# Token transform in 64-row array tiles, one gate product, grouped small VectorE operations and a second recurrence PSUM buffer in a gated spectral/state-space kernel

## The chip, the cores and the metric

The kernel runs on one core of a Trainium2 chip. The core has a matrix engine (TensorE, PE in the profile; its weight loads are PEld), VectorE (DVE), ScalarE (ACT), GpSimd (POOL) and SyncE (SP, which here only issues DMAs). Compute engines read and write SBUF, 128 partitions wide; TensorE writes PSUM, which has 8 banks of 2 KB per partition. The metric is device time in microseconds (us).

## The reference, cut to what matters

```python
S, D = 2048, 1024                      # tokens, channels (batch 1, bf16)
g = sigmoid((x * gate_w).sum(-1))      # one gate per token
a = irfft2(rfft2(x) * (w_r + 1j*w_i))  # 2-D transform over tokens and channels
Lb = exp(exp(log_dt) * (Lambda_re + 1j*Lambda_im))         # 1024 states
Bu = x @ (((Lb - 1)/Lam)[:, None] * (B_re + 1j*B_im)).T
h[t] = Lb * h[t-1] + Bu[t]                                 # 2048 steps
b = 2*real(h @ (C_re + 1j*C_im).T) + x * Dskip
out = g*a + (1 - g)*b
```

The weights `w` have 513 columns, and the transform's column 0 carries the real sums of the two ends of the spectrum packed together, so it takes a small path of its own.

## The kernel before

**Two branches on one instruction stream.** The source is an order written out by hand: the instructions of TensorE, VectorE and ScalarE run in the order in which the Python code issues them, and a generator for each branch is stepped so that the two interleave.

**Front (iterations j = 0 to 15, function `front`).** The token rows are dealt to 128 partitions as token = 16·p + j, so tile j holds the tokens with residue j modulo 16. For each j, `turn_x` transposes the tile by eight matmuls into a one-bank PSUM tile `pt` (L647), and ScalarE copies it into `xQ` (L648). `fold` adds and subtracts its halves on VectorE (L652, L653), `fd` does the channel transform by eight 512-column matmuls (L335), ScalarE copies that out as `X1` (L338), and `s1` does the token transform over the 128 partitions by four matmuls of 512 columns (L344 to L347). VectorE (j below 10) or ScalarE (later) copies the result out as `A1`, one of four buffers (L349), a DMA writes it to DRAM scratch, and VectorE keeps its column 0 in `Acol` (`keep_A1`, L356). The transposes run ahead and end with j = 6. Meanwhile `make_tab` builds the rotation tables on VectorE, ScalarE and GpSimd, and the loads of B and C are issued on SyncE.

**Recurrence (`unit(c, q)`).** Time is cut in 8 chunks c of 256 tokens, the states in halves q. A unit is two steps ("halves", real and imaginary part) of 32 matmuls of 256 columns each (L300, stationary operand B, moving operand columns of `xQ`), each evacuated by ScalarE into `h` (L302). Then VectorE works on the unit: rotate back (L261, L262), join (L267, L268, carry at L270), two scans (L274), carry on (L280 to L282), rotate on (L286, L287, L292, L293). These pieces go into a list, and `vector(us)` issues as many of them as a budget written in the code allows. `early(tb)` multiplies finished states with C for a tile of 128 tokens (L561, with the skip product at L565), ScalarE scales by 1 - g (L579), and the result goes to DRAM. The units and early tiles follow the list `ssm`; from j = 8 on, each front iteration takes one half.

**PSUM.** `psA` (two buffers of two banks) serves the transform. In the front, `psF` (one buffer of two banks) holds the recurrence product and `psX` (two buffers of one bank) the transposes and the gate. After j = 15 both are closed and `psU` (two buffers of two banks) takes the place of both.

**Gate.** At j = 9, 11, 13 and 15, `gate` forms four token tiles' gate sums, 32 matmuls of one column each (L689, stationary operand `xQ`), ScalarE copies four columns (L691), and at the end two GpSimd DMAs bring them to the token order (L693, L695). `gate_end` applies the sigmoid (L699) and makes g and 1 - g (L700 to L705).

**Behind the front.** `Acol` goes to DRAM and back as `Bcol` by two GpSimd DMAs (L362, L365); four 16-column matmuls (L410 to L413) do the rest of column 0's transform. Then 16 steps of the second token stage (L453), the product with w (L461, L462 on VectorE), and the way back (L477, L478), each with one half of the recurrence; then 16 steps of L502, and at last the channel transform back (L592) with the remaining units and the output tiles (`own`, `late_tile`).

Of the kernel before, what the change touches and what calls it, by code (L numbers as in the profile page):

```python
# [13 lines left out]
FP32 = mybir.dt.float32  # L14
# [5 lines left out]
S = 2048  # L20
# [16 lines left out]
def _host_consts():  # L37
# [21 lines left out]
    s1 = np.arange(P)[:, None, None]  # L59
    s2 = np.arange(16)[None, :, None]  # L60
    m1 = np.arange(P)[None, None, :]
    angT = 2 * np.pi * (((16 * s1 + s2) * m1) % S) / S
    Tc, Ts = np.cos(angT), np.sin(angT)
    p = np.arange(P)
    q = p // 8
    a = p % 8
    angK = 2 * np.pi * ((q[:, None] * q[None, :]) % 16) / 16
    delta = (a[:, None] == a[None, :]).astype(np.float64)
    Kc, Ks = delta * np.cos(angK), delta * np.sin(angK)
    f = np.arange(P)  # L70
    fs, fr, fa = f[:, None] // 8, (f[:, None] // 4) % 2, f[:, None] % 4
    hr, hm, ha = f[None, :] // 64, (f[None, :] // 4) % 16, f[None, :] % 4
    angF = 2 * np.pi * ((fs * hm) % 16) / 16
# [14 lines left out]
    for h in range(2):  # L88
# [10 lines left out]
        T3=b16(np.stack([Tc, Ts, -Ts], axis=2)),  # L99
        K3=b16(np.stack([Kc, Ks, -Ks], axis=1)),  # L100
# [7 lines left out]
def kernel(  # L108
# [24 lines left out]
    cT3 = nc.inline_tensor(hc["T3"], name="c_T3").ap()  # L133
# [7 lines left out]
    turn1_dram = dram.tile([16, 2, P, K], BF16, name="turn1_scratch")  # L141
    turn2_dram = dram.tile([32, P, K], BF16, name="turn2_scratch")
    col0_dram = dram.tile([P, 16, 2], BF16, name="col0_scratch")
    z_dram = dram.tile([P, 16], FP32, name="z_scratch")
# [47 lines left out]
    fft["T3"] = raw.rearrange("p (j t m) -> p j t m", t=3, m=P)  # L192
# [4 lines left out]
    def load_T3(a, b):  # L197
        nc.sync.dma_start(out=fft["T3"][:, a:b], in_=cT3[:, a:b])

# [50 lines left out]
    work = []  # L250

    def unit(c, q):
# [24 lines left out]
        def carry_on():  # L277
            if c + 1 < NCH:
                gl = u[:, :, :, TC - 1]
                nc.vector.tensor_mul(out=ck[:, 0, :, js], in0=gl, in1=cTC[:, js].unsqueeze(1).to_broadcast([P, 2, 4]))  # L280
                nc.vector.tensor_mul(out=ck[:, 1, :, js], in0=gl[:, ::-1], in1=sTC2[:, :, js])
                nc.vector.tensor_add(out=carry[:, :, js], in0=ck[:, 0, :, js], in1=ck[:, 1, :, js])  # L282
# [13 lines left out]
        for ri in range(2):  # L296
            psu = pools["u"].tile([P, 4, TC], FP32, name="psu", tag="psu")
            for j in range(4):
                for d8 in range(8):
                    nc.tensor.matmul(psu[:, j, :], lhsT=BT[4 * q + j][:, ri, d8, :],  # L300
                                     rhs=xQ[:, d8, :, 16 * c:16 * (c + 1)], start=(d8 == 0), stop=(d8 == 7))
            nc.scalar.copy(out=u[:, ri].rearrange("p b (q j) -> p b q j", j=16),  # L302
                           in_=psu.rearrange("p b (j q) -> p b q j", j=16))
            if ri == 1:
                work.extend([(2.4, turn_back), (1.5, join), (2.3, lambda: scan(0)), (2.3, lambda: scan(1)),
                             (0.5, carry_on), (2.4, turn), (1.4, join_on)])
            yield 3.5
# [19 lines left out]
    def gfnet():  # L327
        T3_sb, G_sb = fft["T3"], fft["G"]
        Acol = fx.tile([P, 16, 2], BF16, name="Acol")
# [11 lines left out]
        def s1(j):  # L341
            X1 = X1s.pop(j)
            psa = psA.tile([P, 2, K], FP32, name="ps_s1", tag="ps")
            nc.tensor.matmul(psa[:, 0, :], lhsT=T3_sb[:, j, 0, :], rhs=X1[:, 0, :], start=True, stop=False)  # L344
            nc.tensor.matmul(psa[:, 0, :], lhsT=T3_sb[:, j, 1, :], rhs=X1[:, 1, :], start=False, stop=True)
            nc.tensor.matmul(psa[:, 1, :], lhsT=T3_sb[:, j, 0, :], rhs=X1[:, 1, :], start=True, stop=False)
            nc.tensor.matmul(psa[:, 1, :], lhsT=T3_sb[:, j, 2, :], rhs=X1[:, 0, :], start=False, stop=True)  # L347
            A1 = gta.tile([P, 2, K], BF16, name="A1", bufs=4)
            (nc.vector.tensor_copy if j < 10 else nc.scalar.copy)(out=A1, in_=psa)  # L349
            A1s[j] = A1  # L350
            nc.sync.dma_start(out=turn1_dram[j].rearrange("r m k -> m r k"), in_=A1)
            if j:
                keep_A1(j - 1)

        def keep_A1(j):
            nc.vector.tensor_copy(out=Acol[:, j, :], in_=A1s[j][:, :, 0])  # L356
# [4 lines left out]
        keep_A1(15)  # L361
        nc.gpsimd.dma_start(out=col0_dram, in_=Acol)  # L362
        Bcol = fx.tile([P, 16, 2], BF16, name="Bcol")
        with nc.allow_non_contiguous_dma(reason="tiny corner turn"):
            nc.gpsimd.dma_start(out=Bcol, in_=col0_dram.rearrange("(a b) j c -> j a b c", a=8))  # L365
# [4 lines left out]
        Kc_sb, Ks_sb, Kns_sb = fft["K3"][:, 0], fft["K3"][:, 1], fft["K3"][:, 2]  # L370
        Wc = fft["Wc"]
        KRS_sb = fft["KRS"]
        t1_v = turn1_dram.rearrange("j r (a b) k -> (j r a) b k", a=4)
# [34 lines left out]
        yield "w"  # L408
        zps = psA.tile([P, 2, 16], FP32, name="zps", tag="ps")
        nc.tensor.matmul(zps[:, 0, :], lhsT=Kc_sb, rhs=Bcol[:, :, 0], start=True, stop=False)  # L410
        nc.tensor.matmul(zps[:, 0, :], lhsT=Ks_sb, rhs=Bcol[:, :, 1], start=False, stop=True)
        nc.tensor.matmul(zps[:, 1, :], lhsT=Kc_sb, rhs=Bcol[:, :, 1], start=True, stop=False)
        nc.tensor.matmul(zps[:, 1, :], lhsT=Kns_sb, rhs=Bcol[:, :, 0], start=False, stop=True)  # L413
# [94 lines left out]
    def after_ia():  # L508
# [7 lines left out]
        fft["wp"] = bctx.enter_context(tc.tile_pool(name="wp", bufs=1, side="right", reuse_waits="tile"))  # L516
        fft["Sel"] = fft["gt"].tile([P, 4, P], BF16, name="Sel_sb", tag="gc1", bufs=2)
# [126 lines left out]
    def turn_x(j):  # L644
# [3 lines left out]
        nc.scalar.copy(out=xQ[:, :, j, :], in_=pt)  # L648
# [6 lines left out]
    idle = gta.tile([P, K], BF16, name="idle", tag="A1", bufs=4)  # L655
# [11 lines left out]
    load_T3(0, 2)  # L667
    load_x(1)
    load_x(2)
    load_T3(2, 8)  # L670
    for i in range(3, 8):
        load_x(i)
    load_T3(8, 16)
# [8 lines left out]
    zsb = cpool.tile([P, 16], FP32, name="zsb")  # L682
    zt = cpool.tile([P, 16], FP32, name="zt")

    def gate(r0, n):
        zps = psX.tile([P, n], FP32, name="zps_g", tag="pt")
        for r in range(r0, r0 + n):
            for d8 in range(8):
                nc.tensor.matmul(zps[:, r - r0:r - r0 + 1], lhsT=xQ[:, d8, r, :], rhs=gwT[:, d8:d8 + 1],  # L689
                                 start=(d8 == 0), stop=(d8 == 7))  # L690
        nc.scalar.copy(out=zsb[:, r0:r0 + n], in_=zps)  # L691
        if r0 + n == 16:
            nc.gpsimd.dma_start(out=z_dram, in_=zsb)  # L693
            with nc.allow_non_contiguous_dma(reason="gate by token tiles"):
                nc.gpsimd.dma_start(out=zt, in_=z_dram.rearrange("(t a) j -> (a j) t", a=8))  # L695
# [14 lines left out]
    fft["K3"] = fx.tile([P, 3, P], BF16, name="K3_sb")  # L710
# [3 lines left out]
    def load_small():  # L714
        nc.sync.dma_start(out=fft["K3"], in_=cK3)
# [28 lines left out]
    def halves(gen, n):  # L744
        for _ in range(n):
            next(gen, None)

    ssm = chain(unit(0, 0), unit(0, 1), unit(1, 0), unit(1, 1),
                unit(2, 0), early(0), unit(2, 1), early(1), unit(3, 0), early(2), unit(3, 1), early(3),
                unit(4, 0), early(4), unit(4, 1), early(5), unit(5, 0), early(6), early(7), unit(5, 1),  # L750
                early(8), unit(6, 0), early(9))

# [208 lines left out]
```

## Time and profile before

Four runs took 347.52 to 353.04 us, median 350.13. The profiled execution took 344.79 us, its span is 343.0 us; the remaining 1.79 us lie around the span.

| what | value |
|---|---|
| profiled execution, its span | 344.79 us, 343.0 us |
| TensorE busy | 330.8 us (96%), granted clock 1.00 |
| VectorE busy | 292.4 us (85%) |
| ScalarE busy | 167.6 us (49%) |
| token transform, L344 to L347 | 64 matmuls of 512 columns |
| gate, L689 | 128 matmuls of 1 column |
| recurrence product, L300 | 1024 matmuls of 256 columns, 116.1 us busy |
| column copies L356 | 16, mean 159 ns |
| carry L280, L281, L282 | 14 each, means 165, 159 and 167 ns |
| diagonal L878 | 8, mean 245 ns |

A matmul's listed duration (379 ns at 512 columns, 273 at 256) is longer than its share of the engine, since matmuls overlap; the distance from one start to the next is what a matmul costs in a stream. A wait named in the profile belongs to the engine that waited, and idle time of an engine that is not the bound costs nothing.

### The profile page before, as it was taken

The page shows a single profiled execution, that of the slowest core. Times are in us where ns is not written, and L with a number is a line of the kernel's source. Part 1 is how long each engine was busy: PE and PEld are TensorE (multiplying, and loading weights), DVE is VectorE, ACT ScalarE, POOL GpSimd, SP SyncE. Part 2 cuts the span into 40 slices and gives each one's busy share as a digit, 9 for nine tenths or more (in the row PEclk, how much of TensorE's full clock was granted, in tenths as well). Part 3 has the DMA queues.
Part 4 walks back from the last instruction along what each step waited for, and adds up shares of the span by engine and source line. Part 5 has one row for each costly group of instructions (what it writes and reads, how often), then busy time and mean ns, then how long its engine had stood idle before and what let it go on. Part 6 is the DMA issues. An engine that isn't in the chain of part 4 may idle for free.

```text
span 343.0 us, 6408 instructions
## 1 busy us (share of the span) xinstructions
PE 330.8 (96%) x2496; PEld 218.6 (64%) x2529; DVE 292.4 (85%) x477; ACT 167.6 (49%) x215; POOL 35.2 (10%) x66
## 2 busy tenths in 40 slices
PE   8989899989999999999999999999999999999995
PEld 3555377667877684756657474595958885665552
DVE  2659777999997999999999999999546999999951
ACT  3698777663332126655656452365633343434410
POOL 1372111100021000000000000000000002112220
PEclk9999999999999999999999999999999999999999
DMA  7999999998874045889999953995501009845694
GB/s 261 414 260 188 219 208 213 189 259 195 265 175 87 8 94 139 235 217 249 268 254 278 233 155 105 240 227 130 160 0 63 1 11 177 153 109 87 113 159 149
DMA packets 83742, 59.55 MB, mean 174 GB/s; under 512 B 54368, under 2 KB 74496, under 8 KB 83584
## 3 DMA queue, kind: packets, MB, share of 16 engines
q1 hardware_dynamic: 80400, 56.46, 63.8%
q0 software_dynamic: 3232, 2.67, 8.0%
q8 instruction: 20, 0.33, 0.4%
q14 instruction: 10, 0.08, 0.1%
q10 hardware_dynamic: 80, 0.01, 0.0%
HBM read 31.32 MB, written 17.84 MB: 143 GB/s over the span
## 4 chain that ended last, share of the span: by engine, by line
PE 82%; ACT 6%; DVE 6%; issue 3%; DMA 2%; SPq 0%; ACTq 0%; DVEq 0%
PE psu L300 30%; PE ps_y L561 26%; PE ps_fd L335 4%; PE ps_h L561 4%; PE ps_id L592 4%; PE ps_is L477 2%; PE ps_is L502 2%; PE ps_is L478 2%; DMA G_sb<-c_G 2%; PE ps_y L565 2%; PE ps_s L453 2%; ACT xQ L648 1%; ACT X L338 1%; ACT h L302 1%; PE pt L647 1%
## 5 line engine op out<-in xcount | busy, mean ns | idle before, releaser
L300 PE MATMUL psu<-xQ,BT 128*128 128x256 bf16 x1024 | 116.1, 273 | 2.0 <-ACT zsb L691 1.0
L300 PEld LDWEIGHTS <-BT 128*128 128x128 bf16 x1024 | 99.5, 98 | 17.7 <-issue 2.9
L561 PE MATMUL ps_y<-CT,h 128*128 128x512 bf16 x436 | 99.5, 379 | 0.6
L561 PEld LDWEIGHTS <-h 128*128 128x128 bf16 x512 | 49.5, 98 | 55.3
L274 DVE TENSOR_TENSOR_SCAN h<-rz,h 128x1024 bf16<-128x1024 f32 x32 | 72.4, 2282 | 0.3
L302 ACT CAST h<-psu 128x1024 bf16<-128x1024 f32 x32 | 32.3, 1010 | 58.5 <-PE psu L300 58.5
L607 POOL DMA_DIRECT2D BT<-y_scratch x10 | 12.1, 1206 | 212.6 <-ACT BT L595 178.7
L335 PE MATMUL ps_fd<-G_sb,preT 128*128 128x512 bf16 x119 | 29.6, 379 | 2.4 <-ACT X L338 1.6
L579 ACT ACTIVATE ye<-ps_y,omg 128x512 f32<-128x512 f32 x20 | 12.6, 683 | 33.1 <-PE ps_y L565 22.7
L261 DVE TENSOR_TENSOR su<-h,tab 128x2048 bf16<-128x2048 bf16 x16 | 19.6, 1223 | 8.0 <-ACT h L302 5.4
L335 PEld LDWEIGHTS <-preT 128*128 128x128 bf16 x128 | 11.9, 97 | 15.3 <-issue 2.7
L455 ACT CAST X<-ps_s 128x1024 bf16<-128x1024 f32 x16 | 16.2, 1014 | 8.7 <-PE ps_s L453 8.7
L262 DVE TENSOR_TENSOR h<-h,tab 128x2048 bf16<-128x2048 bf16 x16 | 19.6, 1225 | 0.8
L338 ACT CAST X<-ps_fd 128x1024 bf16<-128x1024 f32 x16 | 16.2, 1012 | 8.2 <-PE ps_fd L335 6.7
L287 DVE TENSOR_TENSOR h<-h,tab 128x2048 bf16<-128x2048 bf16 x16 | 19.6, 1225 | 0.5
L286 DVE TENSOR_TENSOR sg<-h,tab 128x2048 bf16<-128x2048 bf16 x16 | 19.5, 1218 | 0.0
L504 ACT CAST ZT<-ps_is 128x1024 bf16<-128x1024 f32 x16 | 15.4, 1022 | 5.2 <-issue 3.0
L648 ACT COPY xQ<-pt 128x1024 bf16<-128x1024 bf16 x16 | 15.9, 1019 | 1.7 <-PE pt L647 1.7
L349 DVE CAST A<-ps_s 128x1024 bf16<-128x1024 f32 x10 | 12.2, 1220 | 5.2 <-PE ps_s L347 5.2
L480 ACT CAST C<-ps_is 128x1024 bf16<-128x1024 f32 x16 | 16.1, 1007 | 0.0
L592 PE MATMUL ps_id<-raw,ZT 128*128 128x256 bf16 x128 | 15.9, 273 | 0.0
L561 PE MATMUL ps_h<-CT,h 128*128 128x512 bf16 x62 | 14.4, 379 | 0.1
(192 smaller groups left out, 388.6 us busy)
## 6 DMA issues: line engine op xcount, KB each, us to landing
y_scratch<-ye SPq DMA_DIRECT2D x20, 256.0 KB, 2.7
CT<-in_A_x_dram SPq DMA_DIRECT2D x8, 512.0 KB, 6.1
turn_scratch<-A SPq DMA_DIRECT2D x16, 256.0 KB, 3.2
Bb<-turn_scratch SPq DMA_DIRECT2D x16, 256.0 KB, 4.0
turn_scratch<-C SPq DMA_DIRECT2D x16, 256.0 KB, 2.9
raw<-turn_scratch SPq DMA_DIRECT2D x16, 256.0 KB, 3.9
Wb<-in_A_w_r_dram SPq DMA_DIRECT2D x32, 127.8 KB, 4.0
Wb<-in_A_w_i_dram SPq DMA_DIRECT2D x32, 127.8 KB, 3.7
```

What stands on the lines that cost most here:

```text
L261: nc.vector.tensor_mul(out=su, in0=u[:, ::-1], in1=bc(1))
L262: nc.vector.tensor_mul(out=u, in0=u, in1=bc(0))
L274: nc.vector.tensor_tensor_scan(out=seg, data0=rz[:, js].rearrange("p j t -> p (j t)"), data1=seg, initial=0.0, op0=ALU.mult, op1=ALU.add)
L286: nc.vector.tensor_mul(out=sg, in0=u[:, ::-1], in1=bc(3))
L287: nc.vector.tensor_mul(out=u, in0=u, in1=bc(2))
L300: nc.tensor.matmul(psu[:, j, :], lhsT=BT[4 * q + j][:, ri, d8, :], rhs=xQ[:, d8, :, 16 * c:16 * (c + 1)], start=(d8 == 0), stop=(d8 == 7))
L302: nc.scalar.copy(out=u[:, ri].rearrange("p b (q j) -> p b q j", j=16), in_=psu.rearrange("p b (j q) -> p b q j", j=16))
L335: nc.tensor.matmul(ps[:, cls, :], lhsT=preTs[j][:, 4 * cls + d4, :], rhs=G_sb[:, cls, d4, :], start=(d4 == 0), stop=(d4 == 3))
L338: nc.scalar.copy(out=X1.rearrange("p r (i c) -> p r i c", c=2), in_=ps.rearrange("p c (r i) -> p r i c", r=2))
L561: nc.tensor.matmul(psy, lhsT=hs[c, jb // 4][:, ri, jb % 4, P * tq:P * (tq + 1)], rhs=CT[ri][:, jb, 512 * dh:512 * (dh + 1)], start=(i == 0 ...
L592: nc.tensor.matmul(pse[:, slot, :], lhsT=ZT_t[:, i, tb, :], rhs=fft["Gi"][:, i, :], start=(kb == 0), stop=(kb == 1))
L648: nc.scalar.copy(out=xQ[:, :, j, :], in_=pt)
```

## The change

**Token transform.** The 2048-point transform over tokens is split 32 x 64 where it was 16 x 128. `turn_x` writes `xQ` with the partition order (p = 2·q + g) sorted as g·64 + q, so the two halves of the partitions hold two residue classes. `s1` still issues four 512-column matmuls for a j, but each contracts over 64 partitions, rows 0 to 63 for g = 0 and 64 to 127 for g = 1 (`tile_position` (0, 0) and (64, 0)), into two PSUM banks. The real and imaginary output share the 128 columns. The constants shrink from three to two 128-column blocks for each j. The recurrence reads `xQ` with runs of 8 elements (16 bytes) where it read runs of 16.

**A1.** The four buffers become one tile with four slots; ScalarE copies from j = 8 on. `keep_A1` copies column 0 of all four slots at once, at j = 4, 8, 12 and behind the front; it is issued behind the copy of the next j, so its first slot then holds the tile of the next group.

**Column 0.** The way of `Acol` over DRAM is replaced by a transpose on TensorE (32 output partitions), two VectorE operations and 16 matmuls of 16 columns over 32 partitions.

**Gate.** One product at j = 10: the gate weights are spread to 32 columns, and 32 matmuls of 512 columns write four 32-partition strips of one bank (`tile_position` (0, 32·i)). ScalarE copies 512 columns, and the two DMAs follow at once; the first reads 4 partitions in pieces of 16 bytes.

**VectorE.** The carry takes two operations where it took three, the diagonal one where it took eight.

**Order.** `psF` and `psX` are closed after j = 11 and `psU` opened there. In `ssm`, `unit(5, 1)` comes before `early(7)`, and `unit(6, 1)` is taken in behind `unit(6, 0)`, ahead of `early(8)` and `early(9)`.

```diff
 def s1(j):
-    nc.tensor.matmul(psa[:, 0, :], lhsT=T3_sb[:, j, 0, :], rhs=X1[:, 0, :], start=True, stop=False)
-    nc.tensor.matmul(psa[:, 0, :], lhsT=T3_sb[:, j, 1, :], rhs=X1[:, 1, :], start=False, stop=True)
-    nc.tensor.matmul(psa[:, 1, :], lhsT=T3_sb[:, j, 0, :], rhs=X1[:, 1, :], start=True, stop=False)
-    nc.tensor.matmul(psa[:, 1, :], lhsT=T3_sb[:, j, 2, :], rhs=X1[:, 0, :], start=False, stop=True)
-    A1 = gta.tile([P, 2, K], BF16, name="A1", bufs=4)
-    (nc.vector.tensor_copy if j < 10 else nc.scalar.copy)(out=A1, in_=psa)
+    for r in range(2):
+        for g in range(2):
+            half = slice(64 * g, 64 * (g + 1))
+            nc.tensor.matmul(psa[:, g, :], lhsT=T2_sb[half, j, r, :], rhs=X1[half, r, :],
+                             start=(r == 0), stop=(r == 1), tile_position=(64 * g, 0))
+    A1 = A1_4[:, j % 4]
+    (nc.vector.tensor_copy if j < 8 else nc.scalar.copy)(out=A1, in_=psa)
...
-    if j:
-        keep_A1(j - 1)
+    if j % 4 == 0 and j:
+        keep_A1(j - 4)
...
 def keep_A1(j):
-    nc.vector.tensor_copy(out=Acol[:, j, :], in_=A1s[j][:, :, 0])
+    nc.vector.tensor_copy(out=Acol[:, :, j:j + 4].rearrange("p g j -> p j g"), in_=A1_4[:, :, :, 0])
...
-keep_A1(15)
-nc.gpsimd.dma_start(out=col0_dram, in_=Acol)
...
-    nc.gpsimd.dma_start(out=Bcol, in_=col0_dram.rearrange("(a b) j c -> j a b c", a=8))
+keep_A1(12)
...
+aps = psA.tile([32, P], BF16, name="aps", tag="ps")
+nc.tensor.transpose(out=aps, in_=Acol.rearrange("p g j -> p (g j)"), identity=ident)
+nc.vector.tensor_copy(out=Bcol[:, 0:2].rearrange("j c a b -> j (c a b)"), in_=aps)
+nc.vector.tensor_scalar_mul(out=Bcol[:, 2], in0=Bcol[:, 0], scalar1=-1.0)
+yield "a"
...
+    for i in range(8):
+        lhs, r = parts[i // 4]
+        nc.tensor.matmul(zps[:, c, :], lhsT=lhs[:, i % 4, :], rhs=Bcol[:, r, i % 4, :], start=(i == 0), stop=(i == 7))
...
+x_t = xQ.rearrange("p d j (g q) -> p d g j q", g=2)
...
-    rhs=xQ[:, d8, :, 16 * c:16 * (c + 1)], start=(d8 == 0), stop=(d8 == 7))
+    rhs=x_t[:, d8, :, :, 8 * c:8 * (c + 1)], start=(d8 == 0), stop=(d8 == 7))
...
-nc.scalar.copy(out=xQ[:, :, j, :], in_=pt)
+nc.scalar.copy(out=xQ[:, :, j, :].rearrange("p d (g q) -> p d g q", g=2), in_=pt.rearrange("p d (q g) -> p d g q", g=2))
...
-def gate(r0, n):
-    zps = psX.tile([P, n], FP32, name="zps_g", tag="pt")
-    for r in range(r0, r0 + n):
-        for d8 in range(8):
-            nc.tensor.matmul(zps[:, r - r0:r - r0 + 1], lhsT=xQ[:, d8, r, :], rhs=gwT[:, d8:d8 + 1],
-                             start=(d8 == 0), stop=(d8 == 7))
+def gate():
+    zps = psX.tile([P, K], FP32, name="zps_g", tag="pt")
+    for d8 in range(8):
+        for i in range(4):
+            nc.tensor.matmul(zps[32 * i:32 * (i + 1), :], lhsT=gw32[:, d8, :], rhs=xQ[:, d8, 4 * i:4 * (i + 1), :],
+                             start=(d8 == 0), stop=(d8 == 7), tile_position=(0, 32 * i))
...
+        nc.gpsimd.dma_start(out=z_dram.rearrange("(n i j) -> i n j", i=4, j=4),
+                            in_=zsb[0:P:32, :].rearrange("i (n j) -> i n j", j=4))
+        nc.gpsimd.dma_start(out=zt, in_=z_dram.rearrange("(t p) -> p t", p=P))
...
-nc.vector.tensor_mul(out=ck[:, 0, :, js], in0=gl, in1=cTC[:, js].unsqueeze(1).to_broadcast([P, 2, 4]))
-nc.vector.tensor_mul(out=ck[:, 1, :, js], in0=gl[:, ::-1], in1=sTC2[:, :, js])
-nc.vector.tensor_add(out=carry[:, :, js], in0=ck[:, 0, :, js], in1=ck[:, 1, :, js])
+nc.vector.tensor_mul(out=ck[:, :, :, js], in0=gl.unsqueeze(1).to_broadcast([P, 2, 2, 4]), in1=rot[:, :, :, js])
+nc.vector.tensor_add(out=carry[:, :, js], in0=ck[:, :, 0, js], in1=ck[:, :, 1, js])
...
-for d8 in range(8):
-    nc.vector.tensor_scalar_mul(out=fft["dgD"][:, d8, :], in0=ident, scalar1=dskT[:, d8:d8 + 1])
+nc.vector.tensor_mul(out=fft["dgD"], in0=ident.unsqueeze(1).to_broadcast([P, 8, P]),
+                     in1=vecT[:, 3].unsqueeze(2).to_broadcast([P, 8, P]))
...
-            unit(4, 0), early(4), unit(4, 1), early(5), unit(5, 0), early(6), early(7), unit(5, 1),
-            early(8), unit(6, 0), early(9))
+            unit(4, 0), early(4), unit(4, 1), early(5), unit(5, 0), early(6), unit(5, 1), early(7),
+            unit(6, 0), unit(6, 1), early(8), early(9))
...
-    if j in (9, 11, 13, 15):
-        gate(2 * (j - 9), 4)
+    if j == 10:
+        gate()
...
+    if j == 11:
+        xctx.close()
+        pools["u"] = ctx.enter_context(tc.tile_pool(name="psU", bufs=2, space=PSUM, reuse_waits="tile"))
```

## The prediction

> **What bounds the kernel now.** The page first: busy shares, then the chain of work that ended last.
>
> ```profile
> PE 330.8 (96%) x2496; PEld 218.6 (64%) x2529; DVE 292.4 (85%) x477; ACT 167.6 (49%) x215; POOL 35.2 (10%) x66
> ...
> PE 82%; ACT 6%; DVE 6%; issue 3%; DMA 2%; SPq 0%; ACTq 0%; DVEq 0%
> ```
>
> TensorE is busy for 96% and carries 82% of the chain. But the share is a mean over stages, so the busy time of each engine by stretch comes next (after the stretch and its length: PE, PEld, DVE, ACT, POOL, each with its instruction count, then granted clock, DMA share, GB/s).
>
> ```profile
> 20.00:30.00 10.00, 8.66 (x69) 4.99 (x69) 7.50 (x29) 9.06 (x13) 6.90 (x11) 1.00 1.14 188
> 30.00:40.00 10.00, 8.91 (x58) 4.62 (x58) 7.80 (x19) 9.23 (x14) 2.20 (x4) 1.00 1.10 207
> ...
> 60.00:70.00 10.00, 8.95 (x85) 5.97 (x85) 9.93 (x18) 6.78 (x13) 2.19 (x4) 1.00 1.08 203
> ...
> 160.00:180.00 20.00, 19.89 (x133) 12.59 (x134) 19.54 (x26) 11.89 (x19) 0.00 (x0) 1.00 0.98 260
> ```
>
> From 20 to 40 us ScalarE is the fullest engine (9.06 and 9.23 of 10), ahead of TensorE. From 40 us on TensorE has no gaps worth naming, so there a microsecond of matmuls saved is a microsecond of span. VectorE is nearly as full (19.54 of 20), so it must keep pace. TensorE's own waits up to 130 us, and its order of time around the 12th front iteration, name the gaps (start, length, what, count, and in brackets the idle time before):
>
> ```profile
> PE ps_fd L335 <- ACT X L338: 1.6, 2, 1.3
> ...
> PE psu L300 <- ACT zsb L691: 1.0, 1, 1.0
> ```
>
> ```profile
> 65.50 0.94 PE L689 MATMUL zps_g<-vecT,xQ 128*128 128x1 bf16 x32
> 66.31 1.89 PE L335 MATMUL ps_fd<-G_sb,preT 128*128 128x512 bf16 x7
> 68.03 0.38 PE L344 MATMUL ps_s<-X,raw 128*128 128x512 bf16 x1
> 68.25 0.38 PE L345 MATMUL ps_s<-X,raw 128*128 128x512 bf16 x1
> 68.46 0.38 PE L346 MATMUL ps_s<-X,raw 128*128 128x512 bf16 x1
> 68.68 0.38 PE L347 MATMUL ps_s<-X,raw 128*128 128x512 bf16 x1
> 70.08 3.65 PE L300 MATMUL psu<-xQ,BT 128*128 128x256 bf16 x32 [1.02 <-ACT zsb L691]
> ```
>
> Starts 0.216 us apart are what a 512-column matmul costs in a stream (the listed 0.38 overlaps the next). The last line is a wait for the one recurrence buffer. Everything below is measured against the profiled execution, 344.79 us (343.0 of span and 1.79 around it).
>
> **Token transform (s1).** Before, four matmuls are 4 x 0.216 = 0.86 us for a j. After, four again, each on half of the rows; whether the two halves run at the same time no row here shows. If they do, a j takes 2 x 0.216 = 0.43 us, if not 0.86. Each j also enters and leaves another shape of the array. One row has such a change, the five 8-row transposes of the small vectors (L787), which the program places in a 32-row tile:
>
> ```profile
> 8.34 0.59 PE L335 MATMUL ps_fd<-G_sb,preT 128*128 128x512 bf16 x2
> 8.87 0.28 PE L787 MATMUL vps<-ident,vec 8*128 8x8 bf16 x5
> 9.07 0.39 PE L335 MATMUL ps_fd<-G_sb,preT 128*128 128x512 bf16 x1
> ```
>
> The last L335 before it starts at 8.34 + 0.59 - 0.38 = 8.55, so the next start was due at 8.77 and came at 8.87: 0.10 late. The fifth transpose starts near 8.99 and L335 follows at 9.07, about 0.06 more than their own spacing of 0.03. I take 0.16 us for a way in and out. Then s1 costs 0.43 + 0.16 = 0.59, saving 0.27 a j. Ends: 0.43 saved (free change, both halves at once), 0.16 lost (one after the other). I take 0.27, because the shape change is the measured row, and half of the array idle is the reason for such a tile.
>
> The Trainium skill speaks against the saving: the page "TensorEngine Tiling (Array Packing)", section "Tiling Modes", states that a change of tiling mode drains the engine. Taken as the overlap lost each way, 0.379 - 0.216 = 0.163 us, a j would pay 0.33 and save 0.10, and the forecast below would lose 16 x 0.17 = 2.7 us; L787 shows half of that, so I stay with the row.
>
> Eight of the sixteen lie in the front's ScalarE-bound part. There 8 x 0.27 = 2.2 us are offered; ScalarE idles 0.94 + 0.77 = 1.7 us from 20 to 40, and some of that is waiting for TensorE. I count 0.8 (ends 0 and 2.2). The other eight give 2.2.
>
> **Gate.** The four blocks take 0.80 us each (65.50 to 66.31): 3.2 us. The new product is 32 matmuls of 512 columns. Four strips at once make 8 x 0.216 + 0.16 = 1.9 us, a saving of 1.3; one after the other 32 x 0.216 + 0.16 = 7.1, a loss of 3.9. I take 1.3, by the same choice as for s1. The page "TensorE: Matmul & The Clock Gate", Part 3, reports 3.07 times for four row tiles of 512 columns; 32 x 0.216 / 3.07 would make 2.3 and the saving 0.8.
>
> **Column 0.** Four small matmuls (0.03 apart, 0.1 us) become 16 and a transpose (0.5 + 0.06) with two changes of shape (0.32): 0.8 us lost, ends 0.4 and 1.0. The two GpSimd DMAs that go were long done when needed.
>
> **Waits.** The 1.02 us at 70.08 and 0.24 at 87.80 are for the one recurrence buffer. The new pool's first buffer lies on the old one's banks, so the step at j = 12 waits for the same copy; but the gate's product now stands before it, and by my walk through the order the copy is done by then. In exchange A1 for j = 8 moves into ScalarE's queue ahead of the first h copy (0.9 us by L349's row), which ended at 48.7 while TensorE reached the next step at 49.04. That step would now be ready at 48.5 and wait until about 49.7, 1.2 us. Behind A1 stand the table operations and h in ScalarE's queue, and VectorE's first unit waits for h. Together: 0.1 us gained, ends -1 and +1.3.
>
> **VectorE** is off the end's path as long as it keeps pace, and the margin is thin:
>
> ```profile
> 131.99 0.69 DVE L462 TENSOR_TENSOR X<-X,Wb 128x1024 bf16<-128x1024 bf16 x1
> ```
>
> TensorE needs this product at 133.79 (first L477), 1.1 us after it ends. VectorE gains the 1.72 us that it waits for the sigmoid at 108 (the gate's DMAs now land 30 us earlier), about 0.75 at the first unit (it starts at 55.22 on an h copy that a late table operation holds up; A1 of j = 9 no longer stands in front of that), five carries of 0.09, five column copies of 0.07, 0.2 on the diagonal, and pays 0.25 for Bcol: 3.2, with the front's 0.8 about 4.0. TensorE comes 3.6 earlier, so the cover holds. If it didn't, TensorE would wait at L477. The two GpSimd gate DMAs now stand ahead of the last table copies (L220, L226), which turn_back of the second unit waits for. Issue 0.6 and 1.2, landing 4.0 by their rows, copies 1.4 and 0.8: done near 73, needed near 75.
>
> **Order at the end.** `unit(6, 1)` moves ahead of 14 us of early tiles. It fills VectorE's two idle spells of 5.2 and 5.4 us at 245 to 260, in which TensorE was busy anyway. Nothing waits on VectorE there, so I count 0. The DMA volume falls by 0.5 MB in the front; TensorE waited there only 0.7 us for a load of x; 0.
>
> **The sum.** 0.8 + 2.2 + 1.3 - 0.8 + 0.1 = 3.6 us: 341.2 of 344.79, ratio 0.990. The median of the runs before is 350.13, 1.5% above the profiled one; with the ratio it becomes **346.5 us**. Runs of this kernel lie up to 0.8% on either side of their median; 2% is about what a measurement can tell from no change.
>
> **Rivals.**
>
> *Slower: the tiles run one after the other.* Place: s1 and the gate. Price: 16 x 0.16 + 3.9 + 0.8 = 7.3 us, 352.1, by the ratio 357.5. It decides when a j of s1 takes over 0.90 us (0.86 plus a sixteenth of what the gate then leaves). For it: no row shows two tiles at once. Against: the matmuls alternate between the tiles and write different banks. 0.14.
>
> *Slower: the 16-byte runs.* The recurrence product reads runs of 8 elements. 32 matmuls take 3.49 us with runs of 16, 0.109 each, and the contiguous 256-column L592 takes the same (8 in 0.875), so halving the run from whole to 16 cost nothing, which speaks against. Each nanosecond would cost 1.02 us; at 0.120 the time is 344.79 - 3.6 + 11.3 = 352.5, by the ratio 357.9. "SBUF — State Buffer", section "Door 1: The DMA port swizzle", puts lines at 16 bytes and asks two hits in each, which a run of 8 bf16 meets; no run here shows it. 0.10.
>
> *Faster: shape changes are free.* 16 x 0.43 + 1.5 - 0.4 + 1.3 = 9.3 us, 335.5, by the ratio 340.7. Against: L787, ScalarE in the front, and VectorE, which by its own gain and margin lets only 4.0 + 1.1 = 5.1 us through (344.9). 0.28.
>
> *VectorE takes over.* GpSimd's table copies come 3 us late or the h copies slip, VectorE's gain falls to about 1, and TensorE waits at L477: 1.0 + 1.1 let through, 348.0. 0.10.
>
> **Chances.** Forecast 0.38. Within 2%: 0.38 + 0.10 = 0.48. Faster by over 2%: 0.28. Slower: 0.14 + 0.10 = 0.24. The range runs from the fast rival less some run spread, 339.5, to the slow ones' centre, 357.6, which leaves out about half of these and little below. The forecast's own range is 343 to 349.
>
> **What would show it.** L348's starts in pairs, then 0.59 us from one j's first to the next work; the gate near 1.9 us; L300 still 0.109; TensorE busy near 327; the sigmoid's wait gone; a wait of about 1 us at the second recurrence step; no wait at the first is1. It would be wrong if the tiles don't overlap, if L300 slows, or if VectorE's first unit starts later than now.

## The result

The changed kernel took 347.58 us (median of 44 runs, 345.42 to 349.81), the kernel before, over 71 runs, 346.18 us (344.68 to 353.04). The ratio is 1.0046, with a 95% interval of 1.0032 to 1.0060: half a per cent slower, where the forecast was 0.990. Ratios here and below leave out runs over 1.5% above the fastest of their kernel, most of which are of the kernel before, so they are not the quotients of the medians. That the forecast time, 346.5 us, lies near the measured one is luck: it was scaled from a median of four runs, 350.13, and from the 346.18 of the 71 runs the same ratio gives 342.6. The profiled execution has a span of 345.3 us, before 343.0.

**TensorE works less and waits more.** The busy shares and the chain of the changed kernel's page, the lines that answer to the first two of before:

```profile
PE 326.3 (94%) x2414; PEld 211.9 (61%) x2446; DVE 289.9 (84%) x447; ACT 169.9 (49%) x214; POOL 33.0 (10%) x64
...
PE 72%; DVE 17%; ACT 5%; SPq 2%; issue 2%; DMA 1%; DVEq 0%; ACTq 0%
```

TensorE's busy time fell from 330.8 to 326.3 us, by 4.5. Its idle time, span less busy, rose from 12.2 to 19.0, by 6.8. The difference is the 2.3 us of span. (Both profiles lack 32 or 33 matmul records; profiles with all of them, of experiments 4 and 1 below, show 332.9 and 328.5 us busy, so both idle times are some 2 us too high and their difference stands.) VectorE's share of the chain went from 6% to 17%: the chain now passes through VectorE for some 60 us. The same shift stands in the stretches (columns as in the lines of before): two of before that were not shown yet, then the changed kernel's.

```profile
40.00:50.00 10.00, 9.57 (x64) 6.32 (x65) 7.73 (x17) 6.39 (x11) 1.22 (x2) 1.00 1.03 216
...
100.00:110.00 10.00, 9.95 (x67) 6.13 (x67) 8.04 (x20) 3.52 (x5) 1.20 (x2) 1.00 0.44 49
```

```profile
20.00:30.00 10.00, 8.32 (x68) 4.73 (x70) 7.97 (x31) 9.34 (x11) 6.21 (x11) 1.00 1.08 150
30.00:40.00 10.00, 7.67 (x57) 3.70 (x56) 6.77 (x14) 8.80 (x13) 1.85 (x4) 1.00 1.15 198
40.00:50.00 10.00, 7.43 (x50) 4.51 (x49) 4.51 (x10) 3.88 (x7) 0.84 (x2) 1.00 1.05 224
50.00:60.00 10.00, 8.26 (x66) 5.83 (x67) 6.84 (x13) 8.52 (x13) 0.98 (x2) 1.00 1.06 193
60.00:70.00 10.00, 9.95 (x95) 6.34 (x94) 9.93 (x16) 7.79 (x15) 2.28 (x2) 1.00 1.09 179
...
100.00:110.00 10.00, 7.62 (x48) 4.12 (x46) 9.65 (x17) 2.51 (x4) 0.00 (x0) 1.00 0.37 105
```

Between 40 and 50 us no engine is full: TensorE 7.43, VectorE 4.51, ScalarE 3.88 of 10 (before, 9.57, 7.73 and 6.39). That is the picture of engines that wait for each other and for something outside. Between 100 and 110 TensorE stands still for 2.4 us, which it did not do before (9.95). Its waits name four of the places:

```profile
PE ps_fd L336 <- ACT X L339: 3.0, 4, 1.6
PE ps_s L348 <- DVE A L351: 2.7, 2, 2.1
PE ps_y L571 <- DVE dgD L883: 2.4, 1, 2.4
PE psu L300 <- ACT h L302: 1.8, 2, 1.6
```

The third is new, and the second cost 0.3 us before. What lies behind the second is read in VectorE's own order of time; the copies of A1 wait for a DMA:

```profile
35.38 1.23 DVE L351 CAST A<-ps_s 128x1024 bf16<-128x1024 f32 x1 [1.35 <-DMA turn_scratch<-A]
...
42.36 1.22 DVE L351 CAST A<-ps_s 128x1024 bf16<-128x1024 f32 x1 [3.27 <-DMA turn_scratch<-A]
```

The DMA is the write of the A1 of four rows before, which must have landed before its place is filled again. Before, with four buffers too, no A1 copy waited for one. The copy of row 7, which goes into the place of row 3, has no wait there:

```profile
39.78 1.21 DVE L349 CAST A<-ps_s 128x1024 bf16<-128x1024 f32 x1
```

SyncE's own order of time shows what changed (start, time on the queue), from the write of row 0 to that of row 3: first before, then after.

```profile
13.13 4.02 SPq L351 DMA_DIRECT2D turn_scratch<-A  x2
17.19 8.23 SPq L205 DMA_TRANSPOSE BT<-in_B_B_re_dram  x4
25.47 2.83 SPq L205 DMA_TRANSPOSE BT<-in_B_B_im_dram  x1
28.40 0.53 SPq L351 DMA_DIRECT2D turn_scratch<-A  x1
28.97 4.00 SPq L205 DMA_TRANSPOSE BT<-in_B_B_im_dram  x3
33.01 3.17 SPq L205 DMA_TRANSPOSE BT<-in_B_B_re_dram  x2
36.28 0.53 SPq L351 DMA_DIRECT2D turn_scratch<-A  x1
```

```profile
12.77 0.39 SPq L353 DMA_DIRECT2D turn_scratch<-A  x1
13.21 7.88 SPq L205 DMA_TRANSPOSE BT<-in_B_B_re_dram  x2
21.19 0.53 SPq L353 DMA_DIRECT2D turn_scratch<-A  x1
21.77 3.28 SPq L205 DMA_TRANSPOSE BT<-in_B_B_re_dram  x2
25.09 6.02 SPq L205 DMA_TRANSPOSE BT<-in_B_B_im_dram  x3
31.21 0.52 SPq L353 DMA_DIRECT2D turn_scratch<-A  x1
31.78 1.28 SPq L205 DMA_TRANSPOSE BT<-in_B_B_im_dram  x1
33.10 6.05 SPq L205 DMA_TRANSPOSE BT<-in_B_B_re_dram  x4
39.25 0.53 SPq L353 DMA_DIRECT2D turn_scratch<-A  x1
```

SyncE is not among the engines whose order is written by hand; a planner orders it, and after the change it put two more loads of B ahead of the write of row j = 2, seven where there were five. The writes of rows 2 and 3 went out 2.8 and 3.0 us later (31.21 and 39.25 for 28.40 and 36.28), and a load of B holds the queue for 1.3 us at the least (four took 6.05 at 33.10). Why the planner chose so is not shown.

**Everything is decided in the first 136 us.** From the first is1 product (the first matmul of the way back, L477 before and L481 after) to the end of the span, before took 343.0 - 133.79 = 209.2 us, after 345.3 - 136.12 = 209.2. The other profiled kernels in the table below take the same, 209.2. Its rows are TensorE's starts (the first unit is VectorE's; the group of 64 matmuls, L300, is two recurrence steps in a row), in us; the span and the ratio of the runs stand below:

| | before | after | seven places | early diagonal | both | both, Bcol early |
|---|---|---|---|---|---|---|
| first recurrence step | 42.96 | 44.18 | 42.25 | 44.48 | 42.05 | 41.73 |
| second step | 49.04 | 52.24 | 49.16 | 52.54 | 48.97 | 48.64 |
| VectorE's first unit | 55.22 | 57.05 | 53.97 | 57.34 | 53.77 | 53.44 |
| the group of 64 matmuls | 92.56 | 91.59 | 88.51 | 91.89 | 88.32 | 87.99 |
| first diagonal matmul | 102.99 | 104.57 | 101.37 | 102.33 | 98.76 | 98.60 |
| first is1 | 133.79 | 136.12 | 134.52 | 134.44 | 131.30 | 130.17 |
| span | 343.0 | 345.3 | 343.7 | 343.6 | 340.5 | 339.4 |
| ratio of the runs | 1 | 1.0046 | 0.9943 | 0.9964 | 0.9886 | 0.9853 |

In the changed kernel TensorE loses 3.2 us by the second step (52.24 for 49.04), has it back and 1.0 more at 92 us, loses 2.5 at the diagonal, and 0.7 on the way of column 0. The column of the seven places holds 1.6 us of a lowered clock behind the diagonal (experiment 3).

### The profile page after: what moved, and what is told of

Its sections match the earlier page's. It is cut to its first block, busy times and chain, and to the rows that moved or that the text cites. A ratio compares the mean times of both kernels' runs of the same rounds, so it can differ in the third digit from the quotient of the medians.

```text
span 345.3 us, 6210 instructions
## 1 busy us (share of the span) xinstructions
PE 326.3 (94%) x2414; PEld 211.9 (61%) x2446; DVE 289.9 (84%) x447; ACT 169.9 (49%) x214; POOL 33.0 (10%) x64
## 4 chain that ended last, share of the span: by engine, by line
PE 72%; DVE 17%; ACT 5%; SPq 2%; issue 2%; DMA 1%; DVEq 0%; ACTq 0%
PE ps_y L567 27%; PE psu L300 23%; PE ps_h L567 4%; DVE h L275 4%; PE ps_id L598 4%; PE ps_is L481 2%; SPq L205 2%; PE ps_is L506 2%; PE ps_is L482 2%; PE ps_y L571 2%; PE ps_fd L336 2%; PE ps_s L457 2%; ACT xQ L654 1%; DVE h L263 1%; DVE h L287 1%
## 5 line engine op out<-in xcount | busy, mean ns | idle before, releaser
L300 PE MATMUL psu<-xQ,BT 128*128 128x256 bf16 x1024 | 116.5, 273 | 2.4 <-ACT h L302 1.8
L300 PEld LDWEIGHTS <-BT 128*128 128x128 bf16 x1024 | 98.8, 98 | 19.3 <-issue 6.1
L336 PE MATMUL ps_fd<-G_sb,preT 128*128 128x512 bf16 x119 | 29.3, 379 | 3.7 <-ACT X L339 3.0
L336 PEld LDWEIGHTS <-preT 128*128 128x128 bf16 x128 | 12.0, 97 | 17.2 <-issue 4.5
L286 DVE TENSOR_TENSOR sg<-h,tab 128x2048 bf16<-128x2048 bf16 x16 | 19.5, 1219 | 0.1
L508 ACT CAST ZT<-ps_is 128x1024 bf16<-128x1024 f32 x16 | 15.5, 1024 | 2.2 <-PE ps_is L506 2.2
L351 DVE CAST A<-ps_s 128x1024 bf16<-128x1024 f32 x8 | 9.8, 1221 | 6.4 <-DMA turn_scratch<-A 4.6
```

What stands on the lines that cost most here:

```text
L286: nc.vector.tensor_mul(out=sg, in0=u[:, ::-1], in1=bc(3))
L336: nc.tensor.matmul(ps[:, cls, :], lhsT=preTs[j][:, 4 * cls + d4, :], rhs=G_sb[:, cls, d4, :], start=(d4 == 0), stop=(d4 == 3))
```

## The experiments

**1. The diagonal product earlier.**

```diff
-            if v == "w" and i == 1:          # behind vector(3.0)
+            if v == "w" and i == 0:          # ahead of halves(ssm, 1)
                 nc.vector.tensor_mul(out=fft["dgD"], ...)
```

> The changed kernel with one edit: the single diagonal product (dgD, 1.22 us on VectorE) is issued two steps of the recurrence earlier, ahead of the second scan at about 98 us instead of behind the turn at 103.3 us. Theory 1 (late VectorE is paid at the first product that TensorE needs from it, and that is the diagonal): the wait of 2.38 us at L571 goes, TensorE then has no gap until the first is1 product, the span falls from 345.3 to about 343, ratio to the kernel before about 0.998 (of 1.0046 for the changed kernel). Rival A (VectorE's lateness is what counts, the diagonal is only the first to show it): the wait comes back at the next product of VectorE (the turned h of chunk 1 or the first is1) with 1.5 us or more, and the ratio stays at 1.002 to 1.005.

Measured: 345.70 us against 346.04, ratio 0.9964 (0.9927 to 1.0). The wait at L571 is gone, and TensorE reaches the first is1 1.7 us sooner than after. Not all of the 2.38 came through: this execution was already 0.3 us late at the group of 64, and a small wait came up behind, for the copy of column 0, in TensorE's order of time:

```profile
102.33 0.39 PE L571 MATMUL ps_y<-dgD,xs 128*128 128x128 bf16 x4
...
110.64 0.54 PE L417 MATMUL zps<-Bcol,K_sb 32*128 32x16 bf16 x16 [0.49 <-DVE Bcol L410]
```

Theory 1 holds, though not its "no gap until the first is1"; rival A, a wait of 1.5 us or more, does not. So VectorE being 2 us late was not the trouble by itself: of all that TensorE takes from it here, only the diagonal and, by half a microsecond, column 0 came too late.

**2. SyncE in the hand order too.**

```diff
-engines={PE, DVE, Activation}
+engines={PE, DVE, Activation, SP}
```

> The changed kernel with SyncE's queue also in the order of the program (one more engine in the hand order), so that the write of A1 of row j stands ahead of the loads of B that the program issues after it; TensorE, VectorE, ScalarE and GpSimd keep their instructions in the same order. Theory 1 (the order on SyncE holds up the A1 copies through the four A1 places): the waits of VectorE at L351 for the write fall from 7.2 us to under 1, the second recurrence step starts near 50 in place of 52.2, VectorE's first unit near 55.5 in place of 57.05, and with VectorE 1.5 to 2 us earlier the wait at the diagonal falls below 1: ratio 0.992 to 1.000. Rival B (ScalarE's copies of A1 for j = 8 and 9 cause the late second step, not the writes): the waits at L351 go, but the second recurrence step still waits 1.2 us or more and the ratio stays within 0.002 of 1.0046. What speaks against a gain: loads of B now stand behind writes that wait for A1, and the rest of SyncE's order changes too.

Measured: 380.09 us, ratio 1.0963 (1.0905 to 1.1021). As a repair it is a failure, since the same order governs SyncE's loads of the second stage, and TensorE's waits are now for those:

```profile
PE ps_s L457 <- DMA Bb<-turn_scratch: 16.2, 12, 2.0
PE ps_is L506 <- DMA raw<-turn_scratch: 9.8, 2, 6.7
```

As a probe of the front it is clean: with the same four places, no A1 copy waits for a write any more, the first two recurrence steps start at 42.21 and 49.12 and VectorE's first unit at 53.93, 3.1 us sooner than after. The ratio I expected was wrong; I had counted "the rest of SyncE's order changes too" as a remark and not as a price.

**3. Seven places for A1**, every queue in its order. With seven, the copy of column 0 also reads its own four rows, where in the changed kernel the first of them is overwritten by then.

```diff
-A1_4 = gta.tile([P, 4, 2, K], ...)
+A1_4 = gta.tile([P, 7, 2, K], ...)
-    A1 = A1_4[:, j % 4]
+    A1 = A1_4[:, j % 7]
-    nc.vector.tensor_copy(out=Acol[:, :, j:j + 4]..., in_=A1_4[:, :, :, 0])
+    for i in range(j, j + 4):
+        nc.vector.tensor_copy(out=Acol[:, :, i], in_=A1_4[:, i % 7, :, 0])
```

> The changed kernel with seven places for A1 in place of four (the four-column copy of column 0 becomes four copies of one column each, some 0.3 us more on VectorE for a group), every queue otherwise in the same order. Theory 1: an A1 copy then needs a place that was written three rows earlier, so the waits at L351 for the write go as in the run with SyncE's order by hand, with the order on SyncE itself unchanged; ratio 0.992 to 1.000. Rival B as there: 1.003 to 1.006.

Measured: 344.38 us, ratio 0.9943 (0.9910 to 0.9975). The front agrees with that of the last run to 0.04 us (42.25, 49.16, 53.97), although SyncE's order is the slow one: two different ways to free an A1 copy from the write four rows before give the same front. (In the changed kernel the copy of column 0 at j = 8 also waits 2.4 us for the row just copied. That wait is still there in experiment 2 and gone here, and the front is the same, so it cost nothing.) Theory 1 holds, rival B does not. But TensorE still waits at the diagonal, in its order of time:

```profile
101.37 0.58 PE L572 MATMUL ps_y<-dgD,xs 128*128 128x128 bf16 x4 [2.26 <-DVE dgD L884]
```

VectorE is here 1.1 us ahead of before (its L286 ahead of the diagonal at 97.70 for 98.76), and TensorE waits as long as in the changed kernel, because it is 4.0 us ahead of before itself (the group of 64 at 88.51 for 92.56). In before the product was ready at 101.15 + 1.38 = 102.53, 0.5 us ahead of its first use:

```profile
101.15 1.38 DVE L878 TENSOR_SCALAR dgD<-ident,vecF 128x128 bf16<-128x128 bf16 x8
```

```profile
102.99 0.39 PE L565 MATMUL ps_y<-dgD,xs 128*128 128x128 bf16 x4
```

So the wait was never VectorE's delay alone. It is a due time: what TensorE gains by then beyond VectorE's own gain and that half microsecond, it leaves there.

The 3.2 us that the front gained over the changed kernel are whole at the first diagonal matmul (101.37 for 104.57), and half of them are gone at the first is1 (134.52 for 136.12). Behind the wait the granted clock fell in this execution, to 0.83 over the stretch where the changed kernel has 1.00, and the 16 matmuls behind the diagonal took 106.64 - 101.75 = 4.89 us where the changed kernel's take 108.24 - 104.79 = 3.45:

```profile
100.00:110.00 10.00, 8.63 (x52) 5.28 (x53) 9.69 (x18) 1.26 (x2) 0.00 (x0) 0.83 0.90 175
```

```profile
101.75 5.05 PE L568 MATMUL ps_y<-CT,h 128*128 128x512 bf16 x16
```

In experiment 2, behind a wait of 2.2 us there, the clock fell in the same way; in the changed kernel's profile, behind 2.4 us, it did not.

**4. The kernel before with the diagonal as one product**, the change's VectorE edit alone.

> The kernel before with one edit, taken from the change: the eight diagonal products of 128 columns become one of 1024 at the same place. Theory 1 (it is VectorE's lateness together with the position that makes the wait): the one product would start at 101.15 and end near 102.4, TensorE needs it at 102.99, no wait; ratio 0.999 to 1.001. Rival C (one product in place of eight is late by itself, since the first four eighths are no longer ready ahead of the rest): a wait of 0.3 us or more at L565 and a ratio of 1.001 or more.

Measured: ratio 0.9993 (0.9956 to 1.0031), no wait at L565. VectorE has the product ready at 102.81 + 1.22 = 104.03, TensorE takes it at 104.64 (this execution runs 1.65 us later throughout). One product in place of eight costs nothing by itself; rival C falls.

**5. Both edits**, one and three together.

> The changed kernel with both edits: seven places for A1 and the diagonal product ahead of the second scan. Theory 1, now in this form: the change's savings are there, but TensorE can use them only up to the next product that it waits for; the writes of A1 held up the front (3.2 us) and the diagonal's place held TensorE at 102 to 105 us (2.3 us), and each repair by itself is partly swallowed at the other. From the run with seven places the 64-matmul group starts at 88.51, from the run with the early diagonal it takes 10.44 us from there to the first diagonal matmul and 32.11 to the first is1: 98.95 and 131.1, 2.7 us ahead of the kernel before. Span 340.2, ratio 0.987. Rival D (VectorE is the bound by then, so that the two gains do not add): a new wait of 1 us or more at Bcol (L418), at the first is1 or at an h, span 342 or more, ratio 0.992 or more.

Measured: 342.89 us, ratio 0.9886 (0.9850 to 0.9922); first diagonal matmul at 98.76 and first is1 at 131.30, where 98.95 and 131.1 were expected. The gains add: at the first is1, 1.7 us of experiment 1 and 3.2 of experiment 3 (1.6 and the 1.6 of its lowered clock) against 4.8 here. So the expectation's "each repair by itself is partly swallowed at the other" is not what the traces show; what was lost in experiment 3 went to the clock. Rival D's wait stays under 1 us, just: 0.93 at Bcol (L418).

**6. Both, and A1 of j = 8 and 9 on VectorE again** (`j < 8` to `j < 10`).

> The kernel with both edits and A1 of j = 8 and 9 copied by VectorE again, as before the change. The prediction's step: ScalarE's copy of A1 ahead of h costs TensorE about 1.2 us at the second recurrence step (measured 1.59, and 0.98 with seven places). If so, that wait goes and the second step starts near 48.2 in place of 49.2; VectorE has 1.2 us more before its first unit, in which it waits 2.8 us for h, so its first unit starts no later than 54. By theory 1 the ratio falls by a further 0.002 to 0.003. Rival E (VectorE's place in the chain matters more than TensorE's): its first unit comes later by 1 us and the ratio does not fall.

Measured: 342.74 us, ratio 0.9882 (0.9842 to 0.9923), no different from the last. The step's mechanism is confirmed: the wait of 0.99 us is gone, the second step starts at 48.11. The gain is not kept: TensorE waits 0.94 us for another h at 68.65, where experiment 5 had no wait, and is at the group of 64 at 88.41, for 88.32. (At 101.12 it also waited 2.1 us for a load of x, as experiment 8 did below.) So the wait that I predicted is real and, by the runs, worth nothing that they can tell.

**7. Tile by tile**, in the changed kernel.

```diff
-for r in range(2):
-    for g in range(2):        # s1: alternate between the two row tiles
+for g in range(2):
+    for r in range(2):
...
-for d8 in range(8):
-    for i in range(4):        # gate: go round the four strips
+for i in range(4):
+    for d8 in range(8):
```

> The changed kernel with one edit in the order of matmuls: s1 does both matmuls of one 64-row tile and then both of the other (in place of alternating), the gate the eight of one 32-column strip and then those of the next. Nothing else moves. If neighbours in TensorE's queue must belong to different tiles to run at once, the gate takes 32 x 0.216 = 6.9 us in place of 1.84 (3 of 4 strips' worth lost, less what overlaps at the three seams) and s1 0.75 to 0.96 us a row in place of 0.64. If TensorE looks ahead in its queue, both stay as they are.

Measured in one run, 348.9 us, too few to judge the whole time (its profile also has the clock lowered between 45 and 50 us, ahead of the stretch read here). In TensorE's order of time of this kernel and of the changed one:

```profile
57.84 0.61 PE L348 MATMUL ps_s<-X,raw 64*128 64x512 bf16 x4
58.38 3.67 PE L300 MATMUL psu<-xQ,BT 128*128 128x256 bf16 x32
61.98 4.54 PE L696 MATMUL zps_g<-xQ,gw 128*32 128x512 bf16 x32
66.45 1.90 PE L336 MATMUL ps_fd<-G_sb,preT 128*128 128x512 bf16 x8
```

```profile
61.69 1.91 PE L696 MATMUL zps_g<-xQ,gw 128*32 128x512 bf16 x32
63.53 1.90 PE L336 MATMUL ps_fd<-G_sb,preT 128*128 128x512 bf16 x7
65.36 0.60 PE L348 MATMUL ps_s<-X,raw 64*128 64x512 bf16 x4
65.90 3.67 PE L300 MATMUL psu<-xQ,BT 128*128 128x256 bf16 x32
```

Neither expectation holds as a whole. The s1 takes 0.54 us to the next start either way (57.84 to 58.38, 65.36 to 65.90). The gate takes 66.45 - 61.98 = 4.47 us in place of 1.84. One after the other it would be 32 x 0.216 = 6.9; the 2.4 us between are 0.8 for each of the three seams. The single records of the trace show how. In the changed kernel the 32 matmuls start in eight groups of four, 0.22 us from group to group and at most 11 ns within one. Here the first matmul of the second strip starts 0.880 us behind the gate's first, 6 ns behind the fifth of the first strip's eight, and so at each seam: the first four of a strip run beside the last four of the one before. So TensorE started matmuls of another tile ahead of up to three older ones that waited for their own tile: enough for groups of two, not for groups of eight. In s1 the two tiles' matmuls start at most 21 ns apart in this order and at most 19 in the other.

**8. Both, with the units at the end as before** (`unit(6, 1)` behind the spectral stage, `early(7)` and `early(8)` earlier).

> The kernel with both edits and the recurrence's units at the end in the order of before (unit(6, 1) after the spectral stage, early(7) and early(8) ahead of it). The prediction's step: the new order fills VectorE's idle spells, in which TensorE was busy anyway, and is worth 0. Then the ratio is that of the run with both edits within 0.002. Rival F (the new order shortens or lengthens the tail): a difference of 1 us or more, and it shows as waits of TensorE after 240 us.

Measured: 342.73 us, ratio 0.9884 (0.9846 to 0.9921). From the first is1 to the end it takes 341.1 - 131.87 = 209.2 us, as with the new order. Rival F falls: the new order at the end is worth nothing. (It came to the first is1 0.6 us later than experiment 5 because the load of x for the first early tile landed late; TensorE waited 1.8 us for it.)

**9. Both, and column 0 one step earlier.**

```diff
-(("w", 4), ("a", 1), ("z", 2), ...)
+(("w", 3), ("a", 2), ("z", 2), ...)    # gate_end stays where it was
```

> The kernel with both edits, and the transpose of column 0 with its two small VectorE copies (Bcol) one recurrence step earlier. Theory 1 (the new column-0 path costs 0.8 us of matmuls as the prediction had it, and the rest of what was lost there is a wait for Bcol, 0.93 us at L418): the wait goes, the first is1 product comes at about 130.4 in place of 131.3, the ratio falls by 0.002 to 0.003 from that of the run with both edits. Rival D (VectorE is full by then, so that the wait moves to the next product): the ratio stays within 0.001, and a wait of like size shows at another line, the load of x for the first early tile (xs) among them.

Measured: 342.30 us, ratio 0.9853 (0.9814 to 0.9892), the wait for Bcol gone and the first is1 at 130.17 (0.33 of the 1.13 us gained on experiment 5 is there already at the group of 64, ahead of the edit):

```profile
98.60 0.40 PE L572 MATMUL ps_y<-dgD,xs 128*128 128x128 bf16 x4
98.93 0.23 PE L409 MATMUL aps<-ident,Acol 128*32 128x128 bf16 x1
...
106.37 0.56 PE L418 MATMUL zps<-Bcol,K_sb 32*128 32x16 bf16 x16
```

TensorE is busy for 326.3 us here, exactly as in the changed kernel, in a span of 339.4 in place of 345.3: the same work, 5.9 us less idle. Theory 1 holds for the trace; by the runs alone, this kernel and experiment 5 can't be told apart (their intervals overlap).

**10. The gate's read on ScalarE's queue**, on top of that, behind the last front step.

> The kernel of the run with Bcol earlier, and the gate's read of its values issued from ScalarE's queue after the last front step, in place of GpSimd's queue ahead of the last two table copies (there it waits 9.5 us for the write to land). The prediction put these DMAs at 4.0 us and the copies at 73; measured 75.2 for the read's issue and 77.5 for the copies, beside which three small VectorE instructions were stretched by 1.5 us. Theory 2 (GpSimd's late copies delay VectorE): the copies end near 66, the turn back of the second unit starts about 1 us earlier. What it is worth depends on where VectorE is waited for: nothing, if TensorE has no wait on VectorE after 60 us but Bcol's; 0.5 to 1 us if it has. My figure: 0 to 0.3 us, ratio within 0.001 of the run with Bcol earlier.

Measured: 342.15 us, ratio 0.9849 (0.9808 to 0.9891). GpSimd's last copies end at 67.4 in place of 72.0, but the second unit starts at 74.09 in place of 74.20, not 1 us sooner. Beside the copies, now at 65.24 to 67.35, two folds took 0.77 and 0.83 us that take 0.42 elsewhere, as at the same place in before, and the turn ahead of the second unit starts 0.9 us later (68.62 for 67.74). Worth nothing, as figured.

## Why the prediction was wrong

The price list of the parts was nearly right, and the walk through the order was wrong in two places. By its own steps:

- **Token transform.** 0.59 us for a j was forecast. In the pair of lines above L348 comes 0.10 late (the last L336 starts at 63.53 + 1.90 - 0.38 = 65.05, the next start was due at 65.26) and the next line 0.54 later: 0.64. The two 64-row halves run at once. Of the 0.86 before, 0.22 are saved a j; the second eight gave 1.8 us where 2.2 stood. The change of shape costs 0.64 - 0.43 = 0.21, where the row gave 0.16. The estimate of 0.33 that I drew from the rule in the Trainium skill's page "TensorEngine Tiling (Array Packing)", section "Tiling Modes", was further off.
- **The front's 0.8.** Without the A1 waits the first step starts at 42.05 (experiment 5), 0.91 before 42.96. In the changed kernel it starts 1.2 later.
- **Gate.** 1.9 forecast, 1.84 measured. That is 6.9 / 1.84 = 3.75 times as fast as four strips one after the other. By estimate the 3.07 that the Trainium skill's page "TensorE: Matmul & The Clock Gate", Part 3, reports for four row tiles would have made 2.25.
- **Column 0.** The matmuls cost 0.16 + 0.49 - 0.1 = 0.55 us more, and with the changes of shape the way from the first diagonal matmul to the first is1 takes 31.55 us for 30.80: 0.75 (0.8 forecast). The new wait for Bcol, up to 0.93, was not in the sum. In the changed kernel it is hidden behind the wait at the diagonal.
- **Waits.** Those of 1.02 and 0.24 us for the one recurrence buffer went, as forecast. The new one at the second step was put at 1.2: 1.59 in the changed kernel, 0.98 with seven places. Without it (experiment 6) the time stayed the same.
- **The failed step: SyncE's order.** "The DMA volume falls ... 0" looked at bytes. What counted was the order in which the writes of A1 and the loads of B leave SyncE's one queue, in a program that leaves that order to a planner. In before the copies of A1 had little to spare: the write of j = 3 went out at 36.28, and with the 3.2 us that such writes took to land (the median) it was done near 39.5, by this estimate 0.3 us ahead of the copy into its place at 39.78. Three microseconds on the queue became 3.1 us of TensorE (second step, 52.24 for the 49.16 of experiment 3).
- **The second failed step: "so the cover holds".** I compared VectorE with TensorE at one product, the first is1, and there it did hold: no profile has a wait at that matmul. The diagonal is due 31 us sooner, and in before it was ready about 0.5 us ahead of its use (eight products from 101.15 on, 1.38 us in all, first use at 102.99). Of the 4.0 us that I gave VectorE, the largest piece, 1.72 at the sigmoid, lies at 108 us, behind the diagonal. What TensorE gained by then beyond VectorE's gain had to end there. The sum of 3.6 us was to be had only with this product moved as well.
- **The gate's DMAs.** 4.0 us to landing was taken from the old row; the new write, of 4 partitions in 16-byte pieces, took 10.3, and the last table copies ended at 77.5 in place of 73. Experiment 10 says that this cost nothing.
- **Order at the end.** 0 forecast, 0 measured.

With both stalls out of the way the first is1 comes 133.79 - 131.30 = 2.5 us sooner than before, with column 0 earlier 3.6, which is the sum that I had forecast (0.3 of it is that execution's earlier front). The rival "VectorE takes over" was nearest in kind: it had GpSimd's copies or the h copies slip, and the wait at L477. The stall came from SyncE and fell at the diagonal.

The version of experiment 9 beats both kernels: by its intervals, 1.1 to 1.9% less than before.

## What to carry to other kernels

A saving on the bounding engine is worth what the next fixed meeting with another engine lets through: list every product that it takes from the second-fullest engine, in order of time, with the time by which each is early, and compare the gain with the smallest of these, not with the one that seems most important. Read the order of every queue that the change can shift, those that a planner sets among them: the program text of the DMAs was hardly touched here, and two loads that changed places with a write cost more than the array tiles saved in the front (3.1 us against 0.9). And repair stalls together before judging the change: against the changed kernel the two repairs gave 1.0 and 0.8% singly and 1.6% together, and singly each left the kernel within 0.6% of the one before, from which the change would have looked worth next to nothing.

## What the runs showed of the hardware

- Two row tiles of 64 partitions run fully at once (four 512-column matmuls in 0.43 us plus 0.21 for the changes of shape; the two tiles' matmuls start at most 19 ns apart), and so do four strips of 32 columns (starts at most 11 ns apart; 1.84 us for 32 matmuls, 3.75 times with the changes of shape).
- The order need not alternate strictly: groups of two cost nothing, groups of eight took the gate from 1.84 to 4.47 us, with four matmuls of each strip beside four of the one before.
- Runs of 8 elements in the moving operand cost nothing: L300 takes 116.5 us of busy time for 1024 matmuls, for 116.1 with runs of 16, and 3.51 us from the first start to the next instruction's for 32 (65.90 to 69.41) where before took 3.49 (62.01 to 65.50).
- A DMA of 8 KB that reads 4 partitions in pieces of 16 bytes took 10.3 us to land in the changed kernel and 7.6, 7.2 and 5.8 in experiments 5, 9 and 10, where the one over 128 partitions took 4.0.
- Beside GpSimd's last table copies VectorE's instructions took longer, in each of these places: in the changed kernel a column copy 0.87 us that takes 0.18 elsewhere, in experiment 10 two folds 0.77 and 0.83 us that take 0.42. What the two engines share is not shown by these runs.
- A wait of TensorE can cost more than its length. Behind the waits of 2.3 and 2.2 us at the diagonal in experiments 3 and 2 the granted clock was 0.50 from 102 to 104 us, and 16 matmuls took 4.89 us for 3.45 in experiment 3; behind 2.4 us in the changed kernel's profile and 2.1 in experiment 6 it stayed at 1.00. The mean granted clock of an execution was 0.995 or less in 27 of 44 of the changed kernel, in 5 of 12 with the early diagonal, in 4 of 12 with seven places and in none of the 30 of experiments 5, 6, 8, 9 and 10. That the waits lower it is what these counts suggest; no run here was made to test it.
